# First-turn scalings on VectorE, routing set-up in steps, list work later in a turn: one edit to a fused RWKV-5 and cosine-router kernel

## The chip, the cores and the metric

The kernel runs on one core of a Trainium2 chip. A core has five engines that run their own instruction streams and wait for each other on semaphores: TensorE (PE, with its weight loads shown apart as PEld), VectorE (DVE), ScalarE (ACT), GpSimd (POOL) and SyncE (SP), whose queue starts most of the transfers. The metric is device time in microseconds (us); lower is better.

## The reference, cut to what matters

There are two parts, one after the other. The first is a linear recurrence over 768 tokens for 4 batches and 8 heads of width 48; the second routes each of the 3072 tokens to one of 8 experts and runs that expert's two-layer network.

```python
for t in range(S):                                   # B=4, H=8, S=768, D=48
    cur = np.einsum('bhd,bhe->bhde', u[None] * kt, vt)
    y[:, :, t] = np.einsum('bhd,bhde->bhe', rt, state + cur)
    state = w[None, :, :, None] * state + np.einsum('bhd,bhe->bhde', kt, vt)
x = y.transpose(0, 2, 1, 3).reshape(B * S, H * D)    # 3072 tokens x 384
logits = (x / |x|) @ (emb / |emb|).T / tau           # 8 experts
expert_idx = argmax(logits); gate = softmax(logits)[expert_idx]
out[mask_e] = gate * (relu(x[mask_e] @ w1[e]) @ w2[e])   # 384 -> 1024 -> 384, per expert
```

Everything is float32.

## The kernel before, in words

**Attention.** The sequence is cut into 6 chunks of 128 tokens. A *turn* is one chunk for two of the four batches, so there are 12 turns (`TURNS`). In a turn, K and R (128 tokens by 8 heads by 48) are multiplied by power tables of the decay (`scale_k`, `scale_r`, lines 311 and 315, with tables `kpow` and `rpow`), turned by TensorE (`turn_in`, L331), copied out of PSUM by ScalarE (`take_in`, L336 and L338), and R once more by VectorE times u (`own_r`, L344). Then 64 small matmuls make the scores (`scores`, L357), VectorE masks them and puts the own-token terms in (`mask` L372, `own_terms` L379), and TensorE multiplies with V (`with_v`, L448) and the state (`with_state`, L467). `outer` (L393) makes the state's update; `turn_y` (L482) turns the result to token rows.

**Order.** The order of work is written out by hand in `attention` with a small planner: `plan.at(time, function, arguments)` collects calls, and `emit` sorts them by planned time. A planned time therefore sets only the order in which instructions go into each engine's stream; the engine runs its stream in that order and waits where a semaphore is not yet there. Turn `t` is planned at `t * P` with `P = 9.4`; work for it that comes ahead is planned from `before = at - P`, so the first turn's is planned at negative times.

**Start.** `build_first` starts the first loads, runs `WAKE` pairs of filler matmuls on constants (L96), makes the decay tables by a scan on VectorE, turns them (L121) and copies them out as `kpow` and `rpow` (L122). `build_consts` then makes masks, index rows and cleared lists. `build_embeddings`, planned at 6.6, normalises the expert embeddings and turns them, with work on ACT, POOL, DVE and PE in a row. POOL runs the scalings of a turn only after the first half of the turn before is scored (`after(k, ins, k.scored)`).

**Routing.** After each chunk, logits (L524) are turned (`turn_logits`, L544), taken (`keep_logits`, L549), used to choose the expert (`choose`), and counted (`ranks`, L608); `placed` (L718) reads ranks, and `values` and `rows_of` (L744) build two factors that `put` (L767) multiplies into the expert's token lists, which `collect` (L778) adds up. The banks for turned logits, ranks and lists are the last 128 columns of PSUM tiles `U[0]` and `U[1]`, whose other columns `outer` writes.

**Experts.** The weights go through the SP queue. In the last turn and after it they are paced: each piece waits for the last TensorE instruction put down before it (`after(k, ins, k.last)`). The first two experts in turn begin early on 256 gathered tokens (`gather` L959, `turn_tile` L979 and L982, `first_layer` L1006); the rest follows in `experts`, with two PSUM banks `U` for the second layer (`layer2`, L1036 and L1044). At the end a branch (`again`, L1309) goes round a long block for inputs that do not fit the fixed capacities. With these inputs the block is skipped.

Of the kernel before, what the change touches and what calls it, by code (L numbers as in the profile page):

```python
# [41 lines left out]
WAKE = 6  # L42
# [32 lines left out]
def build_first(k):  # L75
# [18 lines left out]

    for i in range(WAKE):
        nc.tensor.matmul(k.bank[(6 + i) % 8], k.ones, wide, start=True, stop=True)  # L96
# [21 lines left out]
    for src, dst, bank in ((kp, k.kpow, k.U[0]), (rp, k.rpow, k.U[1])):  # L118
        ps = bank.rearrange("q (p s d) -> q p s d", p=NP, s=2)
        for p in range(NP):  # L120
            nc.tensor.transpose(ps[:, p].rearrange("q s d -> q (s d)"), src[:, p, :], k.ident)  # L121
        nc.vector.tensor_copy(dst.rearrange("q (p s) d -> q p s d", s=2), ps[:, :, :, 0:D])  # L122
    wC = k.aconst.tile([128, NP], F32, name="wC")
    nc.vector.tensor_mul(wC, t[:, :, C - 1], wc)
    k.uw = k.aconst.tile([128, NP], F32, name="uw2")
    nc.vector.tensor_mul(k.uw, uw, wc)
# [11 lines left out]
def numbers(k, name, shape, pattern, base, step):  # L138
    i = k.const.tile(shape, I32, name=f"{name}_i")
    k.nc.gpsimd.iota(i, pattern=pattern, base=base, channel_multiplier=step)  # L140
    f = k.const.tile(shape, F32, name=name)
    k.nc.vector.tensor_copy(f, i)
    return f


def build_consts(k):
    nc, pool = k.nc, k.const

# [9 lines left out]
    for s in range(2):  # L158
        nc.vector.tensor_copy(k.smask[halves(s), :], k.umask[halves(s), halves(s)])
        nc.vector.tensor_copy(k.dmask[halves(s), :], k.ident[halves(s), halves(s)])  # L160
    k.half = pool.tile([128, B], F32, name="half")
    nc.vector.memset(k.half, 0.5)
# [4 lines left out]
    nc.vector.tensor_scalar_add(k.ng[:, :, :, 0], k.token, -float(SKIP))  # L167
    k.rev = numbers(k, "rev", [128, E], [[-1, E]], E, 0)
    k.slot = numbers(k, "slot", [128, 128], [[1, 128]], 0, 0)
    k.index = numbers(k, "index", [128, E], [[1, E]], 0, 0)  # L170
    k.caps = pool.tile([128, E], F32, name="caps")
# [10 lines left out]
    k.level = numbers(k, "level", [128, TM], [[128, TM]], 128, 0)  # L182

    k.cum_oh = pool.tile([128, E, B + 1], F32, name="cum_oh")
    nc.vector.memset(k.cum_oh[:, :, 0:1], 0.0)
# [3 lines left out]
    nc.vector.memset(k.on, 1.0)  # L189
    nc.vector.memset(k.on[:, :, 0:1], 0.0)  # L190
# [3 lines left out]
    nc.vector.memset(k.lists[:, :, 0, :], float(SKIP))  # L194
    nc.vector.memset(k.lists[:, :, 1, :], 0.0)
# [3 lines left out]
    k.take_first = pool.tile([128, EARLY, AHEAD], I32, name="take_first")  # L199

# [15 lines left out]
def build_embeddings(k):  # L216

    nc, pool = k.nc, k.aconst
    emb, tau = k.X[1][0:E, 0], k.tau_col
    sq = k.X[1][0:E, 1]  # L220
    nrm = pool.tile([E, 1], F32, name="emb_nrm")
    nc.scalar.activation(sq, emb, ACT.Square, accum_out=nrm)
    nc.gpsimd.tensor_tensor(out=nrm, in0=nrm, in1=k.half[0:E, 0:1], op=ALU.pow)
    nc.vector.tensor_scalar_add(nrm, nrm, 1e-6)
    nc.vector.reciprocal(nrm, nrm)
    nc.vector.reciprocal(tau, tau)
    wide = scratch(k.YT[0], 0)[0:E].rearrange("x (g c d) -> x g c d", g=4, c=2)
    nc.gpsimd.memset(wide, 0.0)

    nc.vector.tensor_scalar(  # L230
        wide[:, :, :, 0:D], emb.rearrange("x (c g d) -> x g c d", c=2, g=4), nrm, tau, ALU.mult, ALU.mult
    )
    ps = k.bank[6].rearrange("q (g x) -> q g x", g=4)
    k.ent = k.const.tile([128, 4, 32], F32, name="ent")
    nc.gpsimd.memset(k.ent, 0.0)
    for g in range(4):
        nc.tensor.transpose(ps[:, g, 0:E], wide[:, g].rearrange("x c d -> x (c d)"), k.ident[0:E, 0:E])
    nc.vector.tensor_copy(k.ent[:, :, 0:E], ps[:, :, 0:E])

    flat = k.X[2][0:E, 0]  # L240
    nc.vector.tensor_scalar(flat, emb, nrm, tau, ALU.mult, ALU.mult)
    k.ent_rows = k.const.tile([128, NK, E], F32, name="ent_rows")
    ps = k.bank[1].rearrange("q (g x) -> q g x", g=4)
    for m in range(NK):
        nc.tensor.transpose(ps[:, m, 0:E], flat[:, m * 128 : (m + 1) * 128], k.ident[0:E, 0:E])
    nc.vector.tensor_copy(k.ent_rows, ps[:, 0:NK, 0:E])


def rings(k):
# [15 lines left out]
    k.V = ring("V", 4, [128, 2, H, DP], True)  # L265
# [44 lines left out]
def scale_k(k, t, u):  # L310
    k.nc.gpsimd.tensor_mul(of(k.Kw, t)[:, u, :, 0:D], of(k.K, t)[:, u], k.kpow)  # L311


def scale_r(k, t, u):
    ins = k.nc.gpsimd.tensor_mul(of(k.Rw, t)[:, u, :, 0:D], of(k.R, t)[:, u], k.rpow)  # L315
# [249 lines left out]
def choose(k, c, rev=None):  # L565

    nc, p = k.nc, k.rt
    rev = k.rev if rev is None else rev
# [212 lines left out]
def attention(k):  # L781
# [4 lines left out]
    for t in range(TURNS):  # L786
# [6 lines left out]
        for u in range(2):  # L793
            plan.at(before + 1.0 + 2 * u, scale_r, k, t, u)
            plan.at(before + 2.0 + 2 * u, scale_k, k, t, u)
            for which in range(2):
                plan.at(before + 3.3 + 2.35 * u + 0.47 * which, turn_in, k, t, u, which)
                plan.at(before + 3.8 + 2.4 * u + 0.6 * which, take_in, k, t, u, which)
            plan.at(before + 4.0 + 2.6 * u, own_r, k, t, u)
# [30 lines left out]
        if bp == 1 and c < NCH - 1:  # L830
# [4 lines left out]
            if c < NCH - 2:  # L835
                plan.at(then + 4.65, keep_logits, k, c)
# [6 lines left out]
                plan.at(then + 4.65, placed, k, c)  # L843
# [4 lines left out]
                plan.at(then + P + 1.77, put, k, c)  # L848
# [575 lines left out]
```

## Time and profile before

| | us |
|---|---|
| median of 3 runs (444.05 to 451.19) | 449.73 |
| the profiled execution's own time | 451.2 |
| its span in the profile | 449.4 |
| PE busy in the span | 410.8 (91%) |
| DVE busy | 150.4 (33%) |
| POOL busy | 128.2 (29%) |
| ACT busy | 102.4 (23%) |

The span runs from the first to the last recorded instruction; 1.8 us of the execution lie around it. In the page's 40 slices a digit is the busy share in tenths; PEclk is the share of its full clock that TensorE was granted; DMA is the mean busy share of the core's 16 DMA engines. In lists of waits a line names the engine and line that waited, then what ended the wait, then the sum, the number and the longest of these waits. In a timeline a line has start, length, engine, line, operation and tiles, and in brackets the idle time before it with what ended it.

### The profile page before, as it was taken

Reading aid. Unit: us, or ns where it says so; the run is one execution under the profiler, and the core shown is the slowest. Engines: PE = TensorE matmul, PEld = TensorE weight load, DVE = VectorE, ACT = ScalarE, POOL = GpSimd, SP = SyncE. Lnnn points to the kernel's source line nnn. Section 1 sums busy time; section 2 is a strip of 40 time slices with the busy share of each in tenths; the row PEclk is TensorE's granted clock in tenths of the full one; section 3 lists DMA queues with packets and bytes.
Section 4 is the critical chain, followed back from the end, with each engine's and each line's share of the span. In section 5 each row is a group of like instructions: output and inputs, shape, how many; then the busy total and the mean of one; then the engine's idle time right before and its main releaser. Section 6 shows DMA issues by size and latency. Waiting matters only on the chain. (4 is left out here: it accounts for less than half of the span.)

```text
span 449.4 us, 10764 instructions
## 1 busy us (share of the span) xinstructions
PE 410.8 (91%) x4516; PEld 285.6 (64%) x4516; DVE 150.4 (33%) x431; ACT 102.4 (23%) x263; POOL 128.2 (29%) x164
## 2 busy tenths in 40 slices
PE   8869888889899599899999999999999999999992
PEld 3669777778788488785555555555555555555551
DVE  4866477767778661011110210310211021011010
ACT  1316454535453413120002002101200200200200
POOL 4645455645451412501132000031013023201010
PEclk9679999989999989989999999999999999999997
DMA  9956775757214727630734404416135144200001
GB/s 177 208 111 133 172 154 124 158 123 160 58 39 133 233 95 210 216 141 35 258 137 146 140 0 140 154 47 191 56 138 164 35 172 152 110 19 34 0 19 41
DMA packets 94684, 54.29 MB, mean 121 GB/s; under 512 B 77955, under 2 KB 89266, under 8 KB 94626
## 3 DMA queue, kind: packets, MB, share of 16 engines
q1 hardware_dynamic: 88658, 43.67, 35.3%
q0 software_dynamic: 3264, 9.44, 6.0%
q8 instruction: 37, 0.61, 0.6%
q10 hardware_dynamic: 2704, 0.40, 0.5%
q14 instruction: 21, 0.17, 0.1%
HBM read 44.20 MB, written 9.58 MB: 120 GB/s over the span
## 5 line engine op out<-in xcount | busy, mean ns | idle before, releaser
L1023 POOL DMA_INDIRECT out_dram<-y,goes x27 | 26.5, 982 | 209.3 <-DVE y L1022 164.7
L1006 PE MATMUL ps<-xTe,w 128*128 128x384 f32 (+3 forms) x216 | 75.5, 499 | 0.0
L1006 PEld LDWEIGHTS ps<-xTe,w 128*128 128x128 f32 x216 | 41.0, 190 | 31.5 <-issue 11.9
L1022 DVE TENSOR_SCALAR y<-pu,lists_sorted 128x384 f32<-128x384 f32 (+3 forms) x27 | 16.1, 614 | 132.8 <-PE pu L1036 84.9
L1009 ACT ACTIVATE hT<-ps 128x384 f32<-128x384 f32 (+3 forms) x36 | 18.2, 504 | 185.5 <-PE ps L1006 183.9
L1044 PE MATMUL pu<-hT,w 128*128 128x432 f32 (+2 forms) x144 | 51.0, 514 | 0.0
L1036 PE MATMUL pu<-w,hT 128*128 128x384 f32 x144 | 46.9, 486 | 0.0
L1044 PEld LDWEIGHTS pu<-hT,w 128*128 128x128 f32 x144 | 27.1, 190 | 22.0 <-issue 15.3
L1036 PEld LDWEIGHTS pu<-w,hT 128*128 128x128 f32 x144 | 27.2, 190 | 18.6
L959 POOL DMA_INDIRECT G<-xs,take x23 | 23.3, 1011 | 27.8 <-DVE lists_sorted L776 11.2
L315 POOL TENSOR_TENSOR Rw<-R,rpow 128x384 f32<-128x384 f32 x24 | 24.9, 1036 | 22.0 <-PE ps L357 9.1
L1006 PE MATMUL ps<-RT,w 128*128 128x256 f32 (+1 forms) x144 | 28.2, 350 | 1.5 <-ACT R L1009 1.2
L357 PE MATMUL ps<-RT,KT 48*64 48x128 f32 x768 | 27.6, 297 | 0.2 <-DVE RT L344 0.2
L999 DVE COPY xTe<-py 128x384 f32<-128x384 f32 (+3 forms) x18 | 10.0, 568 | 48.2 <-PE py L996 47.7
L1006 PE MATMUL py<-xTe,w 128*128 128x384 f32 (+3 forms) x72 | 26.1, 499 | 0.0
L1006 PEld LDWEIGHTS ps<-RT,w 128*128 128x128 f32 x144 | 23.8, 208 | 3.7 <-ACT R L1009 1.4
L357 PEld LDWEIGHTS ps<-RT,KT 48*64 48x64 f32 x768 | 24.3, 148 | 2.6 <-issue 1.8
L311 POOL TENSOR_TENSOR Kw<-K,kpow 128x384 f32<-128x384 f32 x24 | 25.5, 1064 | 0.0
L338 ACT COPY RT<-ps 128x512 f32<-128x512 f32 x24 | 14.1, 588 | 29.2 <-PE ps L331 28.2
L1047 DVE COPY yT<-pu 128x432 f32<-128x432 f32 (+2 forms) x9 | 5.3, 592 | 45.4 <-PE pu L1044 45.4
L344 DVE TENSOR_TENSOR RT<-ps,uw 128x512 f32<-128x512 f32 x24 | 16.4, 689 | 11.8 <-ACT RT L338 11.6
L1006 PEld LDWEIGHTS py<-xTe,w 128*128 128x128 f32 x72 | 13.7, 190 | 10.5 <-issue 4.0
(237 smaller groups left out, 545.4 us busy)
## 6 DMA issues: line engine op xcount, KB each, us to landing
w<-in_moe_w_dram SPq DMA_DIRECT2D x24, 512.0 KB
w<-in_moe_w_dram SPq DMA_DIRECT2D x32, 384.0 KB
K<-in_k_dram SPq DMA_DIRECT2D x24, 192.0 KB
V<-in_v_dram SPq DMA_DIRECT2D x24, 192.0 KB
xs<-X SPq DMA_DIRECT2D x24, 192.0 KB
R<-in_r_dram SPq DMA_DIRECT2D x22, 192.0 KB
out_dram<-y,goes POOLq DMA_INDIRECT x27, 2.6
R<-in_r_dram ACTq DMA_DIRECT2D x2, 192.0 KB
```

Source lines behind the costliest of these rows:

```text
L311: k.nc.gpsimd.tensor_mul(of(k.Kw, t)[:, u, :, 0:D], of(k.K, t)[:, u], k.kpow)
L315: ins = k.nc.gpsimd.tensor_mul(of(k.Rw, t)[:, u, :, 0:D], of(k.R, t)[:, u], k.rpow)
L338: k.nc.scalar.copy(of(k.RT, t)[:, u, :, :, 0, :], k.turned[u][0].rearrange("q (p s i) -> q p s i", p=NP, s=2))
L344: k.nc.vector.tensor_mul(of(k.RT, t)[:, u, :, :, 1, :], k.turned[u][0].rearrange("q (p s i) -> q p s i", p=NP, s=2), k.uw[:, :, None, None ...
L357: ins = k.nc.tensor.matmul(k.D[2 * u + par][halves(s), p * C : (p + 1) * C], KT[rows, u, p, halves(s)], RT[rows, u, p, s].rearrange("q j i ...
L959: k.nc.gpsimd.indirect_dma_start(out=G[0:n, :], out_offset=None, in_=k.xs[0:rows, :], in_offset=IndirectOffsetOnAxis(ap=(k.take_first if f ...
L1006: k.last = k.nc.tensor.matmul(ps, w1[:, m, f * 128 : (f + 1) * 128], x_of(k, e, m)[:, cols], start=(m == 0), stop=(m == NK - 1))
L1009: k.nc.scalar.activation(h_of(k, e, f)[:, cols], ps, ACT.Relu)
L1022: k.nc.vector.tensor_scalar_mul(y[0:n], ps[0:n], k.lists[0:n, e, 1, t : t + 1])
L1023: k.nc.gpsimd.indirect_dma_start(out=k.out[:, :], out_offset=IndirectOffsetOnAxis(ap=k.goes[0:n, e, t : t + 1], axis=0), in_=y[0:n, :], in ...
L1036: k.nc.tensor.matmul(ps, h_of(k, e, f)[:, t * 128 : (t + 1) * 128], w2[:, f, :], start=(f == 0), stop=(f == NF - 1))
L1044: k.nc.tensor.matmul(ps, w2[:, f, m * 128 : (m + 1) * 128], h_of(k, e, f)[:, 0:n], start=(f == 0), stop=(f == NF - 1))
```

## The change

The change has eight parts, all of order and place; what is computed stays the same.

1. Three pairs of filler matmuls at the start in place of six, and one more pair behind the turning of the decay tables. The masks are made between the turning and the copies of the tables; the two small tables `uw` and `wC` are made later.
2. The scalings of turn 0 are on VectorE, K ahead of R. Other turns stay on POOL.
3. `build_consts` goes from ahead of the plan to planned time 4.95; its clears are on POOL; its five conversions on VectorE become `cast_consts` at 7.4. The clearing of V's padding goes in here too.
4. `build_embeddings` becomes three steps, at 7.0, P + 7.5 and P + 9.0. `decays` goes from P + 6.9 to 2P + 7.6.
5. `keep_logits`, `placed` and `count` go from about 4.65 to about 2.42 in their turn, `put` from 1.77 to 3.25.
6. The three pieces of the second expert's first weights go from 14.2, l + 1.4 and l + 4.0 to l + 1.4, l + 2.7 and l + 4.0 (l = 18.4, from the last turn's start).
7. The second of two late `turn_tile` uses bank `U[1]` where both used `Y[0]`; the second layer takes its two banks in strict alternation over all experts.
8. A branch hint for the skipped block is put ahead of the last `layer2`, and the branch falls through to its block by default.

```diff
-WAKE = 6
+WAKE = 3
...
     for i in range(WAKE):
-        nc.tensor.matmul(k.bank[(6 + i) % 8], k.ones, wide, start=True, stop=True)
+        idle(i)
...
+    idle(WAKE)
+    build_masks(k)
+    for src, dst, bank in tables:
+        ps = bank.rearrange("q (p s d) -> q p s d", p=NP, s=2)
         nc.vector.tensor_copy(dst.rearrange("q (p s) d -> q p s d", s=2), ps[:, :, :, 0:D])
+    k.tables = t, uw
...
 def build_consts(k):
+    nc, pool = k.nc, k.const
+    for V in k.V:
+        nc.gpsimd.memset(V[:, :, :, D:DP], 0.0)
...
+def cast_consts(k):
+    for f, i in k.casts:
+        k.nc.vector.tensor_copy(f, i)
+    k.nc.vector.tensor_scalar_add(k.ng[:, :, :, 0], k.token, -float(SKIP))
...
+def embeddings_a(k):
+    nc = k.nc
+    k.nrm = k.aconst.tile([E, 1], F32, name="emb_nrm")
+    nc.scalar.activation(k.X[1][0:E, 1], k.X[1][0:E, 0], ACT.Square, accum_out=k.nrm)
+    nc.gpsimd.tensor_tensor(out=k.nrm, in0=k.nrm, in1=k.half[0:E, 0:1], op=ALU.pow)
+    nc.gpsimd.tensor_scalar_add(k.nrm, k.nrm, 1e-6)
+    k.wide = scratch(k.YT[2], 0)[0:E].rearrange("x (g c d) -> x g c d", g=4, c=2)
+    nc.gpsimd.memset(k.wide, 0.0)
+    k.ent = k.const.tile([128, 4, 32], F32, name="ent")
+    nc.gpsimd.memset(k.ent, 0.0)
...
 def scale_k(k, t, u):
-    k.nc.gpsimd.tensor_mul(of(k.Kw, t)[:, u, :, 0:D], of(k.K, t)[:, u], k.kpow)
+    q = k.nc.gpsimd if t else k.nc.vector
+    q.tensor_mul(of(k.Kw, t)[:, u, :, 0:D], of(k.K, t)[:, u], k.kpow)
...
-            plan.at(before + 1.0 + 2 * u, scale_r, k, t, u)
-            plan.at(before + 2.0 + 2 * u, scale_k, k, t, u)
...
+                place = which if t else 1 - which
+                plan.at(before + 1.0 + 2 * u + place, scale_k if which else scale_r, k, t, u)
+                plan.at(before + 3.3 + 2.35 * u + 0.47 * place, turn_in, k, t, u, which)
+                plan.at(before + 3.8 + 2.4 * u + 0.6 * place, take_in, k, t, u, which)
+            plan.at(before + (4.0 if t else 5.3) + 2.6 * u, own_r, k, t, u)
...
-                plan.at(then + 4.65, keep_logits, k, c)
+                plan.at(then + 2.42, keep_logits, k, c)
...
-                plan.at(then + 4.65, placed, k, c)
+                plan.at(then + 2.42, placed, k, c)
...
-                plan.at(then + P + 1.77, put, k, c)
+                plan.at(then + P + 3.25, put, k, c)
...
-        (0, 0, 0, 0.5), (0, 0, 1, 5.1), (0, 0, 2, 10.8), (1, 0, 0, 14.2), (1, 0, 1, l + 1.4), (1, 0, 2, l + 4.0),
+        (0, 0, 0, 0.5), (0, 0, 1, 5.1), (0, 0, 2, 10.8), (1, 0, 0, l + 1.4), (1, 0, 1, l + 2.7), (1, 0, 2, l + 4.0),
...
-    plan.at(6.6, build_embeddings, k)
-    plan.at(P + 6.9, decays, k)
+    plan.at(-P + 5.25, tables_u, k)
+    plan.at(4.9, tables_w, k)
+    plan.at(4.95, build_consts, k)
+    plan.at(7.0, embeddings_a, k)
+    plan.at(7.4, cast_consts, k)
+    plan.at(P + 7.5, embeddings_b, k)
+    plan.at(P + 9.0, embeddings_c, k)
+    plan.at(2 * P + 7.6, decays, k)
...
-    ps, r = (k.U[t % 2] if t < AHEAD else k.Y[0]), rows_in(e, t)
+    ps, r = k.U[t % 2] if t < AHEAD else (k.Y[0], k.U[1])[e], rows_in(e, t)
...
+        if e == E - 1:
+            k.tc.mark_branch_hint_location("rest", "LikelyTaken")
         layer2(k, e)
...
-    with tc.If(k.left > 0, preferred_fallthrough_block=False):
+    with tc.If(k.left > 0, label="rest"):
```

`embeddings_b` holds the two reciprocals and two scalings on VectorE, `embeddings_c` the seven small transposes on TensorE and the two copies of their results.

## The prediction, on record before the result was known

> **What bounds the kernel now.** I read the page's busy row first, then the stretches, the waits of TensorE, and the timeline where a wait is long.
>
> ```profile
> PE 410.8 (91%) x4516; PEld 285.6 (64%) x4516; DVE 150.4 (33%) x431; ACT 102.4 (23%) x263; POOL 128.2 (29%) x164
> ```
>
> TensorE is the bound: no other engine is busy for more than a third. So an edit is worth what it takes from TensorE's idle time or slow-clock time. Stretches, the first ones cut where the scores of turns 0 to 3 begin, show where these lie (columns: length; PE, PEld, DVE, ACT, POOL busy; clock; DMA share; GB/s):
>
> ```profile
> 0.00:16.70 16.70, 12.49 (x37) 6.53 (x37) 10.82 (x32) 3.22 (x5) 8.60 (x32) 0.92 0.98 187
> ...
> 28.46:38.88 10.42, 10.42 (x250) 9.74 (x249) 5.50 (x14) 3.64 (x9) 4.46 (x5) 0.70 0.12 23
> 38.88:47.41 8.53, 8.53 (x281) 7.68 (x280) 6.54 (x19) 6.40 (x18) 5.71 (x8) 1.00 0.87 191
> ...
> 91.60:103.00 11.40, 9.76 (x285) 8.89 (x281) 6.88 (x19) 3.21 (x11) 4.58 (x4) 0.85 0.60 129
> ...
> 300.00:442.80 142.80, 138.65 (x454) 81.34 (x452) 17.56 (x31) 15.82 (x32) 26.80 (x27) 1.00 0.26 88
> 442.80:449.40 6.60, 0.00 (x0) 0.00 (x0) 0.00 (x0) 0.00 (x0) 0.00 (x0) 0.61 0.10 36
> ```
>
> The reader is to see three things. Turn 1 takes 10.42 us at clock 0.70 and turn 2 takes 8.53 at full clock, so the start pays for its gaps twice. The experts are solid TensorE work, which nothing here shortens. The last 6.6 us hold no work. TensorE's own waits name the causes:
>
> ```profile
> PE pu L767 <- DVE P L744: 4.3, 4, 1.2
> PE py L237 <- DVE YT L230: 3.0, 1, 3.0
> PE pu L979 <- ACT cum_oh L610: 2.8, 1, 2.8
> PE pu L393 <- DVE full L718: 2.1, 4, 0.6
> PE ps L331 <- POOL Rw L315: 2.1, 2, 1.8
> ...
> PE pu L393 <- DVE lg L549: 1.3, 3, 0.4
> ```
>
> **The start, up to the scores of turn 2.** These lines of the timeline carry it:
>
> ```profile
> 6.67 0.68 DVE L115 TENSOR_TENSOR YT<-YT,mid 128x512 f32<-128x512 f32 x1
> 6.91 0.34 PEld L96 LDWEIGHTS ps<-YT,ones 128*128 128x128 f32 x1 [0.52 <-issue]
> ...
> 9.26 0.14 PEld L121 LDWEIGHTS pu<-ident,YT 128*128 128x128 f32 x1 [0.24 <-issue]
> ...
> 10.33 0.56 DVE L122 COPY kpow<-pu 128x384 f32<-128x384 f32 x1 [2.98 <-PE pu L121]
> ...
> 26.84 0.41 PE L237 MATMUL py<-ident,YT 8*128 8x8 f32 x4 [3.04 <-DVE YT L230]
> ```
>
> *Fillers.* The tables are ready at 7.35 (6.67 + 0.68), but twelve filler instructions hold TensorE to 9.26. Six of them end at 6.91, where the seventh weight load stands. The first table's turning then starts at 6.91 and both end near 8.1. The new filler pair (0.86 at full clock) ends near 9.0, when TensorE has nothing else. Four mask copies come ahead of the table copies on DVE: the one that ran alone took 0.18, those beside POOL's scalings 0.95 to 1.04. POOL is idle now, so about 0.5 in all, hidden under the turning. `kpow` and `rpow` follow at 8.5 and 9.0, in place of 10.9 and 11.35: **2.35 earlier**.
>
> *Scalings.* POOL took four times about 0.97, from 11.44 to 15.32. The nearest DVE rows (128x512 at 0.69, 128x384 copies starting 0.47 apart) give about 0.5 each: 9.0 to 11.0. The bytes that landed put K and R of turn 0 in place by 6.3, so no load is late. ACT's four copies (0.59 each) run behind the turnings and end at 12.6; the second `own_r` (0.69) waits for the last. The first scores can begin at **12.3 in place of 16.7**, and end at 14.4; at full clock they take 1.98 (as at 38.88) in place of 3.69.
>
> *Turn 1's scalings* stay on POOL behind the first half of the scores: 13.4 plus 4 x 0.97 is 17.3 (before, 22.7). The turnings end near 18.0, so turn 1's scores begin at **18.3 in place of 28.5**: the embedding chain, 3.04 and 0.79 of TensorE idle, no longer stands in between. K and R of turn 1 land by 11, of turn 2 by 17.
>
> *What is late next.* POOL's stream now holds `build_consts` (2.55 by its rows: four V clears 1.06, index rows and caps 1.05, the moved clears about 0.4), the state's decay (0.82) and `embeddings_a` (pow 0.56, add 0.15, clears 0.63) between the scalings of turns 1 and 2: 17.3 + 2.55 + 0.82 + 1.34 = 22.0. The first scaling of turn 2 is done at 23.0, but TensorE is there at 21.4: 1.6 idle, and 0.5 more for the next. Then the two scalings of `embeddings_b` (0.46 for the row that ran alone) and reciprocals stand on DVE behind `own_r`, and the seven transposes (0.87) stand ahead of the scores on TensorE: about 2.0. Without a clock loss turn 2's scores begin at 30.0.
>
> *The clock.* The Trainium skill, "TensorE: Matmul & The Clock Gate", section "Why this matters for your kernels", asks for 4 us or more of unbroken work to reach full clock and no idle gap over about 3 us to keep it. Fewer fillers are against its first half, yet six still give 1.63 to 6.91, 5.3 us. Its second half does not fit the row 91.60:103.00: clock 0.85 there, and no gap over 1.2 us. The idle share of about a third of a 3.4 us stretch was enough. By the rule, my gaps of 1.6 and 0.5 us cost no clock, but the lists' gaps below cost none either; by the row, one half-clock stretch (1.7 us of work lost) follows the POOL gap. I take the row: **31.7 in place of 38.9, a gain of 7.2** (bounds 3.5, if both slow stretches stay, and 10.5, with neither wait). `cast_consts` (about 1.3 on DVE) falls while turn 1's scores run; a late mask is needed only a turn later.
>
> **The lists.** `put` waited 4.3 for P, built late on DVE: at 3.25 the state's matmuls (1.6 us) go ahead of it and P is there. The last of the four (0.8) lies in the last turn, where DVE's chain of choices sets the end, so I count 3.5. `outer` waited 1.3 for `lg` and 2.1 for `full`, as they share U's banks; both reads now lie behind a mask on DVE. The first is gained whole. In the turns with `placed`, the 0.39 us of DVE delays `own_terms`, which the second half of `with_v` needs at that moment: of 2.1 I count 0.5. The half-clock stretch in 91.60:103.00 (0.15 x 11.4 is 1.7 of lost work) stands behind a `put` gap and goes. Sum **7.0** (bounds 3.3, if DVE takes the place of each wait, and 9). `collect` keeps its place, after `own_terms`, and is done before `outer` comes.
>
> **Weights, banks, branch.** The 2.8 us wait in the last turn is named ACT, but what TensorE waits for is a gathered tile: its transfer begins 1.6 us after its issue, beside a 512 KB piece of weights issued at 150.72. Moved behind the early layer, that piece is gone. Of 2.8, about 1.0 is gained, for ranks stand next on TensorE and need DVE's `counts` at 155.5 (bounds 0 and 2.5). The three pieces take 2.1 us each from 162 on, so the last lands near 168.5, and the second expert starts near 171: no new wait. Two bank changes take the waits of 0.7 and 0.7: 1.3.
>
> At the end, POOL's branch stands after the last landing: it is taken at 445.2, POOL's next instruction is at 448.2. With the block as fall-through the taken branch is the first one, at 441.6 under the last scatter, whose landing POOL awaits until 444.65. The skill's "Runtime: NRT & Kernel Launch", section "Instruction fetch mechanics", says a taken branch outside the fetched window costs a fetch and knows no hint; by that rule alone the tail stays 6.6. By the row, 3.0 us of fetch goes under 3.1 us of wait, hint or no hint, and SP's semaphores (to 445.9) are next: **2.6**. If the hint evicts what TensorE needs next it costs 3.3, TensorE's own branch: bounds -0.7 and 2.9.
>
> **The sum.** 7.2 + 7.0 + 1.0 + 1.3 + 2.6 = 19.1, so the span goes from 449.4 to 430.3, and with 1.8 around it the profiled execution from 451.2 to 432.1. The median of the runs shown is 1.5 below that execution; I predict **430.6**. The gaps of 1.7 us near 189, and the slow clock after them, I leave as they are.
>
> **Rivals.** *A, the sum holds* (426 to 436): 0.55. *B, the front is eaten*: POOL's longer stream and DVE take the places of the waits removed, so 3.5 in place of 7.2 and 3.3 in place of 7.0: 430.6 + 7.4 = 438. For it: POOL's and DVE's streams in turns 1 and 2 have no slack. Against: POOL stands idle from 26.6 to 31 now. 0.22. *C, the clock stays full*: three more half-clock stretches (after 31, 157 and 191) go, 1.7 each, and 1.4 more of the gather's wait: 430.6 - 6.5 = 424. For it: these follow gaps. Against: two of the gaps are not touched. 0.13. *D, the change doesn't do what it says*: loads set the start (DMA share 1.03 until 28 us) and the hint's fetch still stands at the end; lists 7.0 and little else: 443. Against: landings lead use by 5 us. 0.06. *E, slower*: with six fillers TensorE is done at 6.91, and a clock window that is not quite full stays at half; if every window of turns 0 to 7 stays at half, each costs 1.7. The gain of 19.1 is gone with 11 windows more than now, about 17 full-clock windows lost to 65 us; up to 85 us it ends near 460. Against: the fillers touch the tables' turning without a gap. 0.04.
>
> **Numbers.** A change of 2% (9 us) is about what a measurement of this kernel can tell from none; that limit is 440.7. A, C and four fifths of B are below it, 0.86; the rest of B, and D, are within it, 0.10; E is 0.04. The range 422 to 439 takes in A, C and most of B.
>
> **What would show it.** Right: `kpow` near 8.5; scores near 12, 18 and 32; no wait of L767 on P nor of L237; a POOL wait of L331 near 22 of 1 to 2 us; clock 1.00 from 35 to 150; the end 3 to 4 us after the last scatter. Wrong: turn 2's scores after 35, DVE waits at L448 in each turn, or the clock below 0.9 in stretches with no gap.

## The result, and the profile after

| us | before | after |
|---|---|---|
| median of 4 runs each | 449.13 (444.05 to 451.19) | 427.28 (425.06 to 431.89) |
| the profiled execution | 451.2 | 427.7 |
| its span | 449.4 | 425.9 |

The ratio is 0.953, with a 95% interval of 0.942 to 0.965: faster. The ratios here and below leave out runs over 1.5% above the fastest of their kernel, here the one of 431.89. The prediction was 430.6 in a range of 422 to 439; the profiled execution was to take 432.1 and took 427.7.

First the page's busy row of the kernel after, and the row of the granted clock over 40 slices.

```profile
PE 399.3 (94%) x4512; PEld 276.7 (65%) x4512; DVE 147.4 (35%) x428; ACT 103.1 (24%) x263; POOL 124.7 (29%) x167
...
PEclk9999999899999899999999999999999999999999
```

TensorE is busy 11.5 us less with the same useful work. Most of that is clock: up to the experts' second layers, the trace of before has seven stretches of 3.41 us at half clock and that of after has two, and the five that went are 8.5 us of lost work. The rest is mainly eight filler instructions where there were twelve. TensorE is idle 12 us less: span less busy time was 38.6 and is 26.6. Only two slices still show a clock below 9.

Now the stretches of after (length; PE, PEld, DVE, ACT, POOL busy; clock; DMA share; GB/s). The first three are cut where the scores of turns 0, 1 and 2 begin, the fourth is turn 2, and the last is what follows the start of the last scatter.

```profile
0.00:11.70 11.70, 8.46 (x36) 4.52 (x36) 8.43 (x23) 3.17 (x5) 2.69 (x14) 1.00 0.93 171
11.70:17.60 5.90, 5.34 (x144) 4.41 (x144) 5.36 (x13) 1.65 (x4) 4.69 (x8) 1.00 0.97 191
17.60:29.60 12.00, 8.87 (x260) 7.47 (x259) 7.57 (x23) 6.45 (x17) 8.52 (x27) 1.00 0.89 175
29.60:38.20 8.60, 8.60 (x285) 7.78 (x284) 6.52 (x18) 5.02 (x14) 5.44 (x7) 1.00 1.03 224
80.00:93.00 13.00, 13.00 (x334) 11.61 (x333) 9.21 (x27) 6.87 (x17) 5.13 (x5) 0.88 0.57 123
...
421.00:425.90 4.90, 0.00 (x0) 0.00 (x0) 0.00 (x0) 0.00 (x0) 0.98 (x1) 0.86 0.12 46
```

The scores of turns 0, 1 and 2 begin at 11.7, 17.6 and 29.6; before, at 16.7, 28.5 and 38.9. The first record of the granted clock in this trace stands at 4.67; the time before it, for which there is no record, counts as 1.00 in the rows above. The fillers' own weight loads show the slow clock up to there: the one at 4.35 takes 0.34, the next 0.19.

```profile
4.35 0.34 PEld L96 LDWEIGHTS ps<-YT,ones 128*128 128x128 f32 x1 [0.52 <-issue]
4.95 0.19 PEld L96 LDWEIGHTS ps<-YT,ones 128*128 128x128 f32 x1 [0.26 <-issue]
```

From 4.67 on it is full through all of the front. Turn 2 itself (8.60) is as long as it was (8.53). At 80 to 93 there is still a slow-clock stretch without an idle moment in it. The end is 4.9 us where it was 7.6 from the scatter's start.

TensorE's waits in after, with the lines whose counterparts led the list of before:

```profile
PE py L500 <- issue: 2.5, 3, 1.8
PE ps L364 <- POOL T L453: 2.2, 1, 2.2
PE ps L364 <- POOL Rw L348: 1.9, 1, 1.9
...
PE pu L1019 <- DMA G<-xs,take_first: 1.6, 2, 0.8
...
PE pu L426 <- issue: 1.2, 1, 1.2
...
PE pu L426 <- DVE lg L582: 0.6, 1, 0.6
...
PE py L272 <- DVE YT L261: 0.6, 1, 0.6
...
PE ps L800 <- DVE P L777: 0.5, 1, 0.5
```

The four waits of `put` for P that made 4.3 are gone (the 0.5 left is a fifth, which before had too), the one of the embeddings' transposes fell from 3.0 to 0.6, and those of `outer` for `full` (2.1) are gone. What leads the list now is in part new: waits in the middle of chains that had none of this size.

The front in detail, from the timeline of after:

```profile
8.51 0.56 DVE L343 TENSOR_TENSOR Kw<-K,kpow 128x384 f32<-128x384 f32 x1
8.99 0.55 DVE L348 TENSOR_TENSOR Rw<-R,rpow 128x384 f32<-128x384 f32 x1
9.12 0.42 PEld L364 LDWEIGHTS ps<-ident,Kw 128*128 128x128 f32 x4 [1.46 <-DVE Kw L343]
...
12.91 1.01 POOL L348 TENSOR_TENSOR Rw<-R,rpow 128x384 f32<-128x384 f32 x1 [9.48 <-PE ps L390]
...
19.31 0.83 POOL L453 TENSOR_TENSOR T<-T,wC 128x384 f32<-128x384 f32 x1
...
21.70 0.98 POOL L348 TENSOR_TENSOR Rw<-R,rpow 128x384 f32<-128x384 f32 x1
...
22.73 0.66 PE L364 MATMUL ps<-ident,Rw 128*128 128x128 f32 x4 [1.91 <-POOL Rw L348]
```

The scalings of turn 0 start 0.47 apart on DVE. Turn 1's stand at 12.9 on POOL behind the first scores, and the first of turn 2 starts at 21.7, after constants, decay and embeddings: the prediction had 22.0, and 1.6 for the wait that is 1.91.

And the last line of after's timeline, the last scatter, whose start and bracket answer to those of before (there 441.78, idle 4.18, ended by POOL's branch in the line before it):

```profile
421.02 0.98 POOL L1063 DMA_INDIRECT out_dram<-y,goes  x1 [4.17 <-DVE y L1062]
```

**Where the 23.5 us of span come from.** Differences between the starts of the same work in the two traces:

| stretch | gain measured | predicted |
|---|---|---|
| start to scores of turn 2 | 9.3 | 7.2 |
| turn 2 to turn 11 | 4.6 | 7.0, with the last turn's share |
| turn 11 to the first layer of the early experts | 1.6 | 1.0 |
| first layer to second layer | 4.3 | 0 |
| second layers to the last scatter | 1.0 | 1.3, with the late `turn_tile` |
| tail | 2.75 | 2.6 |
| sum | 23.5 | 19.1 |

### The profile page after: what moved, and what is told of

Same layout as the page of the kernel before. It is cut to its first block, busy times and chain, and to the rows that moved or that the text cites. A ratio compares the mean times of both kernels' runs of the same rounds, so it can differ in the third digit from the quotient of the medians.

```text
span 425.9 us, 10753 instructions
## 1 busy us (share of the span) xinstructions
PE 399.3 (94%) x4512; PEld 276.7 (65%) x4512; DVE 147.4 (35%) x428; ACT 103.1 (24%) x263; POOL 124.7 (29%) x167
## 5 line engine op out<-in xcount | busy, mean ns | idle before, releaser
L1081 PEld LDWEIGHTS pu<-w,hT 128*128 128x128 f32 x144 | 27.2, 190 | 18.5
L348 POOL TENSOR_TENSOR Rw<-R,rpow 128x384 f32<-128x384 f32 x22 | 22.8, 1036 | 22.7 <-PE ps L390 20.9
L1046 PE MATMUL ps<-RT,w 128*128 128x256 f32 (+1 forms) x144 | 27.1, 340 | 0.4 <-DVE RT L1022 0.4
L390 PE MATMUL ps<-RT,KT 48*64 48x128 f32 x768 | 24.3, 273 | 0.5 <-DVE RT L377 0.5
L1046 PEld LDWEIGHTS ps<-RT,w 128*128 128x128 f32 x144 | 22.6, 197 | 2.5 <-ACT Rw L1049 0.6
L343 POOL TENSOR_TENSOR Kw<-K,kpow 128x384 f32<-128x384 f32 x22 | 23.5, 1066 | 0.0
L390 PEld LDWEIGHTS ps<-RT,KT 48*64 48x64 f32 x768 | 20.9, 133 | 3.1 <-issue 2.1
L364 PE MATMUL ps<-ident,Rw 128*128 128x128 f32 x96 | 15.6, 286 | 4.8 <-POOL T L453 2.2
```

Of the source, the lines that this page charges most:

```text
L343: q.tensor_mul(of(k.Kw, t)[:, u, :, 0:D], of(k.K, t)[:, u], k.kpow)
L348: ins = q.tensor_mul(of(k.Rw, t)[:, u, :, 0:D], of(k.R, t)[:, u], k.rpow)
L364: k.nc.tensor.transpose(bank[:, p * C : (p + 1) * C], pair(src[:, u], p), k.ident)
L390: ins = k.nc.tensor.matmul(k.D[2 * u + par][halves(s), p * C : (p + 1) * C], KT[rows, u, p, halves(s)], RT[rows, u, p, s].rearrange("q j i ...
L1046: k.last = k.nc.tensor.matmul(ps, w1[:, m, f * 128 : (f + 1) * 128], x_of(k, e, m)[:, cols], start=(m == 0), stop=(m == NK - 1))
L1081: k.nc.tensor.matmul(ps, h_of(k, e, f)[:, t * 128 : (t + 1) * 128], w2[:, f, :], start=(f == 0), stop=(f == NF - 1))
```

## Experiments

Each group of kernels ran beside the kernel before on one chip; that kernel's median was 444.6 in the first group (scalings, embeddings, lists, branch), 448.2 in the second (six fillers, set-up later, weights, hint) and 443.85 in the third (the added matmuls, banks, after once more). The ratio to it is what compares over groups; after's own is 0.953, and 0.962 when it was run again in the third. Where two kernels differ by less than their intervals, I read the traces.

### The front: scalings, embeddings, fillers, POOL's load

**Turn 0's scalings back on POOL.**

```diff
-    q = k.nc.gpsimd if t else k.nc.vector
+    q = k.nc.gpsimd                       # in scale_k and scale_r
-                place = which if t else 1 - which
+                place = which
-            plan.at(before + (4.0 if t else 5.3) + 2.6 * u, own_r, k, t, u)
+            plan.at(before + 4.0 + 2.6 * u, own_r, k, t, u)
-    plan.at(-P + 5.25, tables_u, k)
+    plan.at(-P + 3.9, tables_u, k)
```

> The changed kernel with the first turn's scalings back on POOL, R ahead of K. If the sum of the front holds, POOL's four times 0.97 from the tables at 8.5 end near 12.5 in place of 10.5 on VectorE, the first scores begin near 14 in place of 11.7, and all later turns shift by the same 2 to 2.5: about 429.5. Rival: the front's gain is all in the embedding steps, and POOL's longer stream behind turn 1 is late in any case; then turn 2's scores move by under 0.5 and the time stays near 427.3.

Measured: 429.11 (428.78 to 429.94), ratio 0.964 (0.957 to 0.971). Scores of turns 0 and 1 begin at 13.1 and 19.0 in place of 11.7 and 17.6. The choice of engine, with the order that goes with it, is worth **1.4 us**, less than I had expected, since POOL's four copies run 8.56 to 12.44 while TensorE turns each as it comes; only the last is waited for. Of the 5 us that turn 0 gained, 2.9 are the earlier tables (the copy to `kpow` starts at 7.46, before at 10.33), not the engine.

**The three embedding steps at their old place.**

```diff
-    plan.at(7.0, embeddings_a, k)
+    plan.at(6.6, embeddings_a, k)
-    plan.at(P + 7.5, embeddings_b, k)
-    plan.at(P + 9.0, embeddings_c, k)
-    plan.at(2 * P + 7.6, decays, k)
+    plan.at(6.6, embeddings_b, k)
+    plan.at(6.6, embeddings_c, k)
+    plan.at(P + 6.9, decays, k)
```

> The changed kernel with the three embedding steps run in one row at 6.6 of turn 0, and decays back at P + 6.9. If the embedding chain on TensorE's path was the larger part of the front's gain, turn 1's scores begin near 23 in place of 17.6; the wait on POOL before turn 2 (1.9) and the transposes there (0.8) go away in return, so turn 2's scores begin 2.5 to 3.5 later: about 430.5, and 1.7 more if the gap halves the clock. Rival: what was gained at turn 1 is lost again at turn 2 whatever is done (POOL's stream sets the time of turn 2), then 427 to 428.

Measured: 429.07 (427.63 to 429.77), ratio 0.963 (0.956 to 0.969). From the timeline of this kernel, the scaling of the embeddings and the transposes behind it:

```profile
20.77 1.11 DVE L261 TENSOR_SCALAR YT<-X,emb_nrm,tau 8x384 f32<-8x384 f32 x1 [0.36 <-POOL YT L250]
...
21.94 0.59 PE L272 MATMUL py<-ident,YT 8*128 8x8 f32 x4 [4.22 <-DVE YT L261]
```

The old wait of TensorE is back, 4.22 us of it, and turn 1's scores begin at 22.8 in place of 17.6. The wait for `Rw` is gone in exchange, so turn 2 begins 2.7 later, at 32.2, with a slow clock from 20.4 to 27.2. So the split gives 5.2 us at turn 1 and gives half of it back at turn 2, as the prediction's "what is late next" had it.

**Six filler pairs.**

```diff
-WAKE = 3
+WAKE = 6
...
-    idle(WAKE)
+    idle(9)
```

> The changed kernel with six filler pairs ahead of the tables' turning (one more behind it, as now). If the fillers hold the tables back, the turning begins near 9.2 in place of 6.5, the first scores near 14 in place of 11.7, and all turns shift by about 2: 429.5. Rival: VectorE's masks and ScalarE's copies hide it, or the clock is full earlier and longer with more fillers and pays for them: 427 to 428.

Measured: 433.25 (431.76 to 433.68), ratio 0.964 (0.959 to 0.969). The copy to `kpow` starts at 10.16 in place of 7.46 and every turn's scores up to turn 2 begin 2.6 to 2.7 later. In part that is the accident of when the clock rises, here at 6.99: in two kernels with three pairs where it rises as late (7.45 with the lists at their old times, 7.59 with the set-up later) the copy starts at 7.81 and 7.89, so the fillers themselves cost about 2.3. The clock rises at 7.32 in before, and between 4.55 and 7.61 in the twelve traces with three pairs: rival E's ground, that fewer fillers might keep it at half, is not there. Of the other 3 us by which its span is longer than after's, 2.6 lie between turn 11 and the first layer, where its gathers are later (see the weights below); the fillers are not shown as their cause.

**The routing set-up one turn later**, so that POOL has nothing between the scalings of turns 1 and 2 but the clears of V and the decay:

```diff
-    plan.at(4.95, build_consts, k)
-    plan.at(7.0, embeddings_a, k)
-    plan.at(7.4, cast_consts, k)
-    plan.at(P + 7.5, embeddings_b, k)
-    plan.at(P + 9.0, embeddings_c, k)
+    plan.at(4.95, clear_v, k)             # the four clears of V, out of build_consts
+    plan.at(P + 4.95, build_consts, k)
+    plan.at(P + 7.0, embeddings_a, k)
+    plan.at(P + 7.4, cast_consts, k)
+    plan.at(2 * P + 5.5, embeddings_b, k)
+    plan.at(2 * P + 6.6, embeddings_c, k)
```

> The changed kernel with the clearing of V's padding alone left at 4.95 and the rest of the routing set-up one turn later on POOL (index rows and clears at P + 4.95, first embedding step at P + 7.0), the embedding scalings on VectorE at 2P + 5.5, where VectorE waits for outer, and the small transposes ahead of turn_y in turn 2. If POOL's stream is what holds turn 2 back, the waits of L364 on POOL (1.9 and 0.3) and of L272 (0.6) go, turn 2's scores begin 2 to 3 earlier than 29.6, and the time is about 425. Rival: another engine takes the place at once (VectorE's masks, ScalarE's copies), and it stays within 0.7 of 427.3.

Measured: 426.8 (426.47 to 428.43), ratio 0.952 (0.947 to 0.957): not to be told from after's 0.953. TensorE's waits in this kernel (three of its lines are added above these functions):

```profile
PE pu L429 <- issue: 5.0, 4, 1.7
PE py L503 <- issue: 1.8, 3, 1.3
```

The wait for `Rw` is gone and turn 2 begins at 27.3, 2.3 earlier; but turn 3 begins only 0.5 earlier than in after, and stalls that no semaphore explains stand where there had been fewer. A removed wait of 2 us came back as something else. What that is, is the next question.

### The lists, and what took the place of their waits

**The lists' work at its old times.**

```diff
-                plan.at(then + 2.42, keep_logits, k, c)
+                plan.at(then + 4.65, keep_logits, k, c)
-                plan.at(then + 2.42, placed, k, c)
+                plan.at(then + 4.65, placed, k, c)
-                plan.at(then + P + 3.25, put, k, c)
+                plan.at(then + P + 1.77, put, k, c)
-                plan.at(then + 2.43, count, k, c)
+                plan.at(then + 4.64, count, k, c)
```

> The changed kernel with keep_logits, placed, count and put at their old times. By the prediction's sum for the lists (7.0): about 434. By the two traces (scores of turn 11 gained 13.9 where those of turn 2 gained 9.3): 4.6, about 432. Rival: TensorE's own instruction fetches take over; each gap that the lists left gave the fetch time to catch up, so with the gaps back there are fewer stalls named issue on L500, L426 and L364 in the middle turns (5.8 us in the changed kernel, 1.9 before) and the time rises by only 2 to 3: about 430.

Measured: 432.85 (429.96 to 435.19), ratio 0.974 (0.967 to 0.981). TensorE's waits in this kernel:

```profile
PE pu L800 <- DVE P L777: 4.3, 4, 1.2
PE pu L426 <- DVE full L751: 2.0, 4, 0.6
...
PE pu L426 <- DVE lg L582: 1.5, 4, 0.4
```

All three are back to within 0.2 of what they were before. **After once more**, unchanged, as a control in the third group:

> The changed kernel as it is, beside these three on the same chip: 427.3 (425 to 430), as a measure of how far runs of one kernel differ. The gather's wait and the half-clock stretch behind it stay; where else half-clock stretches fall may differ, each worth 1.7.

Measured: 427.25 (424.45 to 430.33), ratio 0.962 (0.954 to 0.971). The stretch from the scores of turn 2 to those of turn 11, one line for each kernel: before, after, the old times, after again.

```profile
38.88:135.90 97.02, 87.06 (x2664) 77.05 (x2663) 68.95 (x201) 49.98 (x138) 52.05 (x62) 0.98 0.57 128
```

```profile
29.57:122.00 92.43, 85.80 (x2668) 76.55 (x2666) 68.94 (x203) 49.22 (x134) 51.72 (x61) 0.98 0.63 140
```

```profile
31.20:125.50 94.30, 85.43 (x2664) 75.85 (x2662) 69.18 (x202) 48.69 (x134) 51.72 (x61) 1.00 0.59 132
```

```profile
29.57:118.50 88.93, 83.82 (x2667) 75.28 (x2665) 69.02 (x203) 48.70 (x134) 51.75 (x61) 1.00 0.67 148
```

The last two have the full clock throughout, so they price the lists' new times alone: 94.30 - 88.93 = **5.4 us**. (After's own 92.43 holds one slow-clock stretch, from 79.8 to 83.2, as before's 97.02 did from 96.1 to 99.5; it was not removed, it lies elsewhere.) Of the idle time, length less PE busy, 8.87 went to 5.11: 3.8 us, though the waits taken away in these turns are 6.8 (P 3.5 without the last turn's, `full` 2.0, `lg` 1.3). The other 1.6 us are busy time, 85.43 against 83.82. So 3.0 of the 6.8 were given back. In the list of TensorE's gaps of 0.4 us and more in the middle of the attention, those that no wait explains sum to 0.6 with the old times, to 1.9 before, to 5.8 in after, and to 4.8 in after again: 4.2 more than with the old times, of which smaller waits that fell make up 1.2. The two largest of after's, from its timeline, with what POOL did before the second:

```profile
43.66 0.53 PE L500 MATMUL py<-RT,Tmid 48*48 48x64 f32 x18 [1.83 <-issue]
...
78.52 0.82 POOL L453 TENSOR_TENSOR T<-T,wC 128x384 f32<-128x384 f32 x1 [2.48 <-DVE T L447]
79.39 0.42 PEld L364 LDWEIGHTS ps<-ident,Rw 128*128 128x128 f32 x4 [2.32 <-POOL T L453]
```

The first breaks a chain of equal small matmuls whose data are long there. The second is put down to POOL's T, but that turning reads `Rw` and not T, so the name only says what ended at that moment (79.34); in after again the same stall is put down to DVE's T (L447). In the trace's list of transfers, a 16 KB fetch on queue q8 (the page's "instruction") runs from 41.41 to 42.45 and ends 1.2 us before the first stall does; one from 77.06 to 78.03 ends 1.4 before the second. A third, 53.30 to 55.19, goes with a stall of 1.24 that ends at 56.81. The Trainium skill, "Runtime: NRT & Kernel Launch", section "Instruction fetch mechanics", says that instructions come in blocks of 16 KB (256 instructions) and that crossing into the next is mostly hidden.

The traces can be asked where in TensorE's stream the stalls stand. Count its recorded instructions in order, weight loads, matmuls and the sequencer's own together:

| kernel | stalls of 0.4 us and more that no wait explains, by the number of the instruction that comes late |
|---|---|
| before | 1730 (1.34), 1985 (0.60) |
| after | 1730 (1.83), 2497 (1.24), 3521 (0.54), 3779 (2.23) |
| after again | 1730 (0.47), 1987 (0.98), 2497 (1.24), 3779 (2.14) |
| old times | 3522 (0.62) |

All are 193 to 195 more than a multiple of 256. From 24 to 134 us the traces of the fourteen kernels have 67 such stalls (those put down to a tile that the late instruction doesn't touch are among them), at different source lines, and all 67 stand there. The fetches on q8 fit the same step: 37 for 9135 recorded instructions in after, 247 each. So each stall stands at **the entry into the next block of TensorE's instructions**, and "mostly hidden" does not hold for these: they cost up to 2.7 us. The fetch itself sets the time: in these traces none of the blocks 1 to 25 (block 0 starts at instruction 193) is entered less than 1.20 us after the end of its fetch, and at the 67 stalls it is 1.20 to 1.62. Why a fetch starts early or late (0.7 us or 3.0 after the block before it is entered) is open. Two kernels tried to move the stalls.

**One long matmul more per turn**, as unused work: 512 columns into a bank of its own in turns 2 to 9. It takes time but almost no instructions, so the fetch was meant to gain on TensorE.

```diff
+def extra(k, t):
+    k.nc.tensor.matmul(
+        k.D[0], k.ones, of(k.AT, t)[:, 0].rearrange("q r n -> q (r n)"), start=True, stop=True,
+        skip_group_check=True,
+    )
...
+        if 2 <= t <= 9:
+            plan.at(at + 6.6, extra, k, t)
+            plan.at(at + 6.85, k.nc.scalar.copy, k.peek[:, 0:1], k.D[0][:, 0:1])
```

> The changed kernel with extra work that nothing uses: in each of turns 2 to 9 one matmul over 512 columns (about 0.9 us of TensorE in four instructions), ahead of turn_y, and a one-column copy on ScalarE behind it. Eight turns give 6.9 us of added TensorE work. If TensorE's stream is held by its instruction fetches, this work gives them time: the stalls named issue (and those of 1 us or more behind a fetch) shrink from about 6 to 2 or 3, and the time grows by only 3 to 4, to about 431. Rival: those stalls have another cause and stay, then the time grows by the whole 6.9, to about 434.

Measured: 432.58 (430.62 to 434.6), ratio 0.970 (0.962 to 0.979); 5.3 above the control. From turn 2 to turn 11 it takes 95.2 in place of 88.9: 6.3 of the 6.9 us of added work. The unexplained stalls sum to 4.4, against 4.8 in the control: they hardly shrank. The count of instructions says why this is no test against the fetch. The added matmuls fall into blocks 4, 7, 9, 11, 14, 16, 18 and 21. The control stalls at the ends of blocks 5, 6, 8 and 13, and this kernel at the ends of these and of 10, and none of them got any added time. In the kernel with the lists at their old times, waits of 0.44, 0.57 and 0.45 do lie in blocks 6, 8 and 13, and the stalls behind these blocks are 0.30, none and 0.37, where the control has 0.98, 1.24 and 2.14.

**Many short matmuls more per turn**, also unused work: 56 of 64x64 in the same place, in time meant to be equal to the long one.

```diff
+def extra(k, t):
+    AT, V = of(k.AT, t), of(k.V, t)
+    for i in range(56):
+        s, h, p = i % 2, i // 2 % 8, i // 16
+        k.nc.tensor.matmul(
+            k.D[0][halves(s), p * HC : (p + 1) * HC], V[halves(s), 0, h, :],
+            AT[halves(s), 0, h % 2, p * HC : (p + 1) * HC],
+            start=True, stop=True, skip_group_check=True,
+        )
```

> The same with the extra 0.8 us of TensorE work as 56 matmuls of 64 by 64 by 64 (about 112 instructions a turn, 14 ns a matmul, 6.4 us in all) in place of one long one. If instruction fetch holds TensorE, the stalls stay or grow, and the time grows by 6.4 and more, 434 to 437. Rival (stalls from another cause): as for the long matmul, 434.

Measured: 454.25 (452.5 to 457.11), ratio 1.022 (1.012 to 1.031). This one missed its aim. From its timeline:

```profile
46.23 0.69 PE L491 MATMUL py<-AT,V 64*64 64x64 f32 x32
...
51.99 3.71 PE L437 MATMUL ps<-AT,V 64*64 64x64 f32 x112
```

The 56 calls leave 112 recorded matmuls, which take 3.71 us, 33 ns each; I had counted 56 at 14. (The first line has 32 of `with_v`, of the same shape, in 0.69 us, 22 ns each; what makes the added ones slower is not shown.) Eight such turns are 29.7 us, against the 27 measured, and with their weight loads they run at 60 instructions a microsecond, where turn 2 of after runs at 66: the stream got thinner, not denser. So it does not test a denser stream. But its trace has 1784 recorded instructions more and 44 fetches on q8 in place of 37, 255 for each, and its three stalls stand at the same steps of 256.

What is shown, then: with the lists at their old times these stalls make 0.6 us, with the new times 4.8 in the control, and they are entries into blocks of instructions. What is not shown is a change that removes them.

### Weights, banks, branch

**The second expert's first weights at their old places.**

```diff
-        ..., (0, 0, 2, 10.8), (1, 0, 0, l + 1.4), (1, 0, 1, l + 2.7), (1, 0, 2, l + 4.0),
+        ..., (0, 0, 2, 10.8), (1, 0, 0, 14.2), (1, 0, 1, l + 1.4), (1, 0, 2, l + 4.0),
```

> The changed kernel with the second expert's first weight pieces at 14.2 and l + 1.4 as before. By the prediction's step (only the gather waits beside that piece): the wait of L1019 grows from 1.6 to about 3 and the time by 1.0, about 428.3. Rival: the gaps near 189 (1.2 and 0.5 on L1006) and the half-clock stretch behind them were its doing too, since they are missing in the changed kernel's trace; then 3 to 4 more, about 431.

Measured: 430.58 (427.43 to 432.15), ratio 0.959 (0.955 to 0.964). Its profiled execution is one of 427.43, no longer than after's. TensorE's wait for the gathered tiles in it:

```profile
PE pu L1019 <- ACT sq L550: 1.3, 1, 1.3
```

That is 1.3 against 1.6 in after: the old pacing alone doesn't bring back the 2.8. Nor does the new pacing keep the wait away: with it, and nothing near it changed, it is 2.65 in the kernel without the hint and 2.5 in the one with six fillers, each with 1.2 more for `cum_oh` behind it. The stretch from first to second layer takes 38.5 us, as in after (38.3; before 42.6). So the new pacing isn't shown to be what removed the gaps near 189, and the median's 3 us more have no place in the trace.

**The banks at their old places.**

```diff
-    ps, r = k.U[t % 2] if t < AHEAD else (k.Y[0], k.U[1])[e], rows_in(e, t)
+    ps, r = k.U[t % 2] if t < AHEAD else k.Y[0], rows_in(e, t)
...
-            ps = next_bank(k)[:, 0:DM]
+            ps = k.U[t % 2][:, 0:DM]          # and the two like it in layer2
```

> The changed kernel with the banks of before: both late turn_tile calls on Y[0], and the second layer starting each expert on U[0]. By the prediction's step the two waits of 0.7 come back, 1.3 in all: about 428.6. Rival: the waits come back but are filled, since the weights or the gathers behind are as late: under 0.5.

Measured: 428.51 (427.87 to 428.71), ratio 0.962 (0.955 to 0.970), 1.3 above the control. Both waits are back:

```profile
PE pu L1081 <- DVE y L1062: 0.7, 1, 0.7
...
PE py L1019 <- DVE RT L1022: 0.6, 1, 0.6
```

Their sum is the 1.3 that the prediction gave; the medians alone could not tell it. In the traces the stretch from the second layers to the last scatter takes 242.06, as in before, where after and the control take 241.09 and 241.08.

**The branch as it was, without the hint.**

```diff
-        if e == E - 1:
-            k.tc.mark_branch_hint_location("rest", "LikelyTaken")
...
-    with tc.If(k.left > 0, label="rest"):
+    with tc.If(k.left > 0, preferred_fallthrough_block=False):
```

> The changed kernel with the branch of before: no hint, and the other block as fall-through. From the last scatter's start to the end 7.6 in place of 4.9, so 2.7 more, about 430, and nothing else moves. Rival: the gain at the end was a matter of when the last landing came, then under 1 us.

Measured: 430.74 (426.3 to 432.93), ratio 0.961 (0.952 to 0.970). A stretch of this kernel, from the last scatter's start to the end of its span:

```profile
422.46:430.20 7.74, 0.00 (x0) 0.00 (x0) 0.00 (x0) 0.00 (x0) 0.98 (x1) 0.73 0.10 34
```

7.8 with the rounding, against 4.9 in after: 2.9 us.

**The hint alone left out**, with the block still as fall-through:

```diff
-        if e == E - 1:
-            k.tc.mark_branch_hint_location("rest", "LikelyTaken")
```

> The changed kernel without the hint, the branch still falling through to its block. In the changed kernel's trace VectorE and POOL still take 2.9 and 2.7 from their branch to the next instruction, hint or not, and it lies under the last scatter's landing. So the fall-through alone gives the gain and the time stays at 427.3 (427 to 428), with TensorE's branch at 3 us again but hidden. Rival: the hint gives the gain, then 430.

Measured: 428.23 (426.96 to 429.75), ratio 0.954 (0.949 to 0.959). Its last scatter in the timeline, in a span of 426.7:

```profile
421.83 0.98 POOL L1063 DMA_INDIRECT out_dram<-y,goes  x1 [4.17 <-DVE y L1062]
```

From there to the end it is 4.83, as in after (4.88). The hint adds nothing that can be seen; the place of the branch does all of it.

## Why the prediction was right, and where not

**The bound.** Right: each microsecond gained is idle time of TensorE, or its fillers, or its slow clock, or the end behind it.

**Fillers and tables.** Right in mechanism, a little short: `kpow` was ready at 8.0 (7.46 and 0.56 for the copy) and the scores began at 11.7 (8.5 and 12.3 predicted). The six pairs cost 2.3 to 2.7, where I had counted 2.35.

**Scalings.** DVE took the 0.5 each that were predicted. As a part by itself the choice of engine was worth 1.4 only.

**What is late next.** Right by place and size: a POOL wait of 1.91 (1.6 predicted), 0.30 for the next (0.5), then the embeddings' transposes; turn 2 at 29.6, where 30.0 stood for the case without a clock loss.

**The front's clock charge failed.** From the row with clock 0.85 I charged one half-clock stretch of 1.7 us behind the POOL gap. In after's trace the clock stays full there, and 7.2 became 9.3. Eleven traces have this gap, of 1.8 to 2.0 us. In four the charge is right: the clock is at half for 3.4 us from 24.5 with the lists at their old times, from 23.3 with the old branch, from 22.7 with the long matmul and from 24.7 with the many short ones. In seven, after and after again among them, it stays full. The changes of clock in each trace lie on steps of 3.41 us from a start that differs from one execution to the next. By after's steps, counted from 4.67, its gap (20.82 to 22.73) is cut by the step at 21.74 into 0.92 and 0.99, and the fuller of the two windows is idle for 1.29 us in all. Over the eleven traces that fuller window is idle for 1.22 to 1.62 us in the seven where the clock stays, and for 1.89 to 2.26 in the four where it halves. The Trainium skill's rule of a 3 us gap ("TensorE: Matmul & The Clock Gate", section "Why this matters for your kernels") was the wrong guide here. But the row was only half a guide: in the trace of before a window from 92.65, idle for 1.20 us, halves the clock, and one from 150.67, idle for 1.75, does not. A gap near half a window costs 1.7 or nothing by the accident of the phase. I should have priced it between. The clock also sets much of the scatter: after again took 424.45 at a mean granted clock of 0.995 and 430.33 at 0.978; 0.017 of 424 is 7 us of clock.

**The lists: the sum was near, its terms were not.** Without the clock the prediction's terms make 5.3 (3.5 for P, 1.3 for `lg`, 0.5 for `full`), and the old times against the control measure 5.4. But of the terms, `full` came whole (2.0, not 0.5), and TensorE's stalls at its instruction blocks grew by 4.2 us (0.6 to 4.8), which the prediction did not foresee. The fourth term, "the half-clock stretch goes", failed in the profiled execution: behind the 2.2 us stall the clock drops at 79.8. In after again it doesn't, and the stretch gained 8.1, not 4.6. So the sign "clock 1.00 from 35 to 150" did not come either: after's clock halves at 79.8 and 141.2.

**First to second layer, 4.3, predicted at nothing.** I left the gaps near 189 (1.19 and 0.52, ended by ACT in before) and the slow clock behind them as they were. In after they are absent, and 38.3 us do the work of 42.6. The old weights' places don't bring them back, and in every later trace the stretch takes 36.8 to 39.5. Their cause is open; it is the largest part of what the prediction missed. That the other terms together make 19.2 against 19.1 predicted is luck: the front gained 2.1 more than predicted and the stretch with the lists 2.4 less.

**Gather, banks, tail.** Before had two waits for gathered tiles, 0.8 and 2.8; after has two of 0.8. So 2.0 went, not 1.0, but the traces speak against the pacing as the cause: with it the wait is 1.6 in some and 2.2 to 2.7 in others, and in the one with the old places it is 1.3. Banks 1.3, confirmed. The tail 2.75, confirmed at 2.9 and 4.83 by two kernels; the cost of the branch is nearly the same and only its cover is new. POOL's branch is taken at 420.78, and the next instruction behind it and the scatter is at 423.50: 2.7 us (3.0 before), all while the scatter is under way. The Trainium skill says that a taken branch whose target is not in the window already fetched must wait for a fetch ("Runtime: NRT & Kernel Launch", section "Instruction fetch mechanics"); that fits, since in before an 8 KB fetch on q14 starts at 445.28, 0.08 us after POOL's branch, though no run isolates it as the cause of the 3 us.

**The rivals.** A holds. B's mechanism is real in part (half of the embedding's gain was eaten at turn 2, and the block stalls took 4.2 us of the lists' gain), but its size is not. C's clock is what the better executions show (424.45 with one half-clock stretch left). D falls with the front and the tail, E with the clock that rises no later with three pairs than with six.

## What to carry to other kernels

Price a removed wait by what TensorE meets next, and after semaphores count its own instruction stream among the candidates: here 4.2 us of new stalls that no semaphore names stand against 6.8 us of removed waits. To know them, number the engine's instructions: stalls that stand at steps of 256, whatever the line, are entries into the next block. In the first turn, put set-up that nothing needs yet behind the chain that everything needs, and check which queue it then blocks one turn later. A taken branch that is put ahead of a wait is hidden by that wait, with no hint.

## What the runs showed of the hardware that I had not expected

- The granted clock changes on steps of 3.41 us whose phase differs between executions. One and the same gap of 1.9 us costs 1.7 us of work (four traces) or nothing (seven).
- All 67 TensorE stalls of 0.4 to 2.7 us that no wait explains, over 24 to 134 us of fourteen traces, stand at steps of 256 recorded instructions, 1.20 to 1.62 us after a 16 KB fetch has ended.
- A run of 112 recorded 64x64 matmuls into one bank took 33 ns each, where `with_v`'s of the same shape took 22.
